# A top-32 threshold from the larger and the smaller of each two scores

## The chip, the cores and the metric

The kernel runs on one core of one Trainium2 chip. The metric is the device time of the whole kernel in microseconds; for the kernel before it is 1531.25 us, the median of 3 runs (1530.28 to 1532.67). A core has five engines that work at the same time, each through its own list of instructions in order: TensorE (PE; the loading of its weights is shown apart as PEld), VectorE (DVE), ScalarE (ACT), GpSimd (POOL), and SyncE (SP), which only starts transfers here. They wait for one another through semaphores. Matrix products land in PSUM; all other tiles lie in SBUF.

## The reference, cut to what matters

```python
def _attn_ref(q, k, v):                      # q, k, v: 8 x 8 x 576 x 64, fp32
    scores = np.matmul(q, k.transpose(0, 1, 3, 2)) / np.sqrt(64)
    kth = np.partition(scores, -32, axis=-1)[..., -32:-31]    # the 32nd largest of each row
    scores = np.where(scores >= kth, scores, -1e9)
    attn = np.exp(scores - np.max(scores, axis=-1, keepdims=True))
    attn = attn / (np.sum(attn, axis=-1, keepdims=True) + 1e-09)
    return np.matmul(attn, v)

def _moe_ref(x, w_in, w_out):                # x: 4608 x 512, w_in: 512 x 2048, w_out: 2048 x 512
    h = x @ w_in
    return (h * np.cos(h)) @ w_out

# reference: attention, heads side by side as 4608 x 512, then _moe_ref
```

For each of 8 x 8 x 576 rows of 576 scores the kernel needs two numbers before it can go on: the largest score and the 32nd largest. Everything below the latter is masked out.

## The kernel before, cut to what matters

A *unit* is 128 rows of tokens for two heads (index `j`), so there are 36 x 4 = 144 units. A unit passes through the engines over several *slots*: in slot `i`, VectorE searches the top 32 of unit `i` (`u`), ScalarE masks and exponentiates unit `i - 1` (`w`), GpSimd normalises unit `i - 2` (`x`), the transfers transpose unit `i - 3` (`y`), and in every second slot TensorE multiplies two older units with the values (`z`). TensorE also makes the scores of unit `i + 1`, and fills its remaining time with the two feed-forward products (`feed`). Each slot gets credit for 4.1 calls of `ff1` or `ff2`. The order of instructions is the program's order. The scores of a unit lie in one PSUM tile of four banks (`sc`, one buffer), and ScalarE copies them to `s` in SBUF.

```python
    def scores(u):
        sc = u["sc"] = ps.tile([P, 2, 2, 512], F32, tag="sc", name="sc", bufs=1)
        for h in range(2):
            for j in range(2):
                d = slice(j * D, (j + 1) * D)
                for b, q0, rows, r0 in u["parts"]:
                    st = pairs[b, u["hp"]]
                    nc.tensor.matmul(
                        sc[r0 : r0 + rows, j, h, 0:HS],
                        st["q"][d, q0 : q0 + rows],
                        st["k"][d, h * HS : (h + 1) * HS],
                        start=True,
                        stop=True,
                    )

    def take_scores(u):
        s = u["s"] = work.tile([P, 2, S], F32, tag="s", name="s", bufs=4)
        nc.scalar.copy(
            out=s.rearrange("p j (h w) -> p (j h) w", h=2),
            in_=u.pop("sc").rearrange("p j h w -> p (j h) w")[:, :, 0:HS],
        )

    def topk_round(u, rnd):
        s = u["s"]
        if rnd == 0:
            u["m8"] = small.tile([P, 2, TOPK], F32, tag="m8", name="m8")
            u["rest"] = work.tile([P, 2, S], F32, tag="rest", name="rest", bufs=1)
        m8, rest = u["m8"], u["rest"]
        src = s if rnd == 0 else rest
        at = slice(8 * rnd, 8 * rnd + 8)
        for j in range(2):
            nc.vector.max(m8[:, j, at], src[:, j])
        if rnd < TOPK // 8 - 1:
            for j in range(2):
                nc.vector.match_replace(rest[:, j], m8[:, j, at], src[:, j], NEG)
        else:
            del u["rest"]

    def bounds(u):

        m8 = u.pop("m8")
        nb = u["nb"] = small.tile([P, 2, 2], F32, tag="nb", name="nb")
        nc.scalar.mul(out=nb, in_=m8[:, :, 0 : TOPK : TOPK - 1], mul=-SCALE)
        nd = u["nd"] = small.tile([P, 2], F32, tag="nd", name="nd")
        for j in range(2):
            nc.scalar.activation(
                out=nd[:, j : j + 1], in_=m8[:, j, TOPK - 1 : TOPK], func=AF.Identity,
                bias=nb[:, j, 0:1], scale=SCALE,
            )
    # ... mask, exponentials, reciprocal, normalise and the rest are cut
```

`nc.vector.max` (MAX8 in the profile) writes the eight largest of a row in descending order. `match_replace` replaces these eight by a very low number; in the profile it is a MATCH_VALUE_LOAD and a MATCH_REPLACE8. Four rounds give the top 32 in order. `bounds` takes the first and the last of the 32.

```python
    def slot(i, u, w, x, y, z):
        if x:
            reciprocal(x)
        if u:
            topk_round(u, 0)
            decode_second(2)
        if w:
            bounds(w)
            mask(w)
            exponentials(w)
        if u:
            topk_round(u, 1)
            topk_round(u, 2)
            topk_round(u, 3)
        take_banks()
        if z:
            values(z)
        if i + 1 < NU:
            scores(units[i + 1])
        if z:
            take_values(z)
        if i + 1 < NU:
            take_scores(units[i + 1])
        for load, b, hp in at_slot.get(i, []):
            load(b, hp)
        load_weights(2)
        if y:
            transposes(y)
        gate(1)
        if x:
            normalise(x)
            split(x)
            write_halves(x)
        feed(2)
        take_banks()
        decode_third()
        decode_first(2)
        reduce_first()
        reduce_second()
        feed(3)
        sines(2)
```

The first 9 slots (`early_slot`) and the last ones (`last_slot`) do the same in another order, without the transfers. `decode_*` are steps on the weights in the first slots. What `feed` calls:

```python
    def ff1(blk, i):
        # ... cut: two blocks of 128 columns, each
            for c in range(NC):
                nc.tensor.matmul(mm[:, at : at + w], w_in[...], blk["xT"][:, c], ...)

    def ff2(blk, i, f0):
        # ... cut
        for f in range(f0, f0 + 2):
            nc.tensor.matmul(o, g[:, at : at + P], w_out[f], start=f == 0, stop=f == NF - 1)
```

Of the kernel before, what the change touches and what calls it, by code (L numbers as in the profile page):

```python
# [10 lines left out]
F32 = mybir.dt.float32  # L11
# [3 lines left out]
AF = mybir.ActivationFunctionType  # L15
ALU = mybir.AluOpType

P = 128
TOPK = 32
NEG = -3.4028234663852886e38  # L20
# [11 lines left out]
def kernel(  # L32
# [9 lines left out]
    nc = tc.nc  # L42
    ctx.enter_context(tc.manual_schedule())
    B, H, D, S = qT.shape
# [6 lines left out]
    HS = S // 2  # L51
    SCALE = 1.0 / math.sqrt(D)
# [3 lines left out]
    consts = ctx.enter_context(tc.tile_pool(name="consts", bufs=1))  # L56
    loads = ctx.enter_context(tc.tile_pool(name="loads", bufs=5))
    work = ctx.enter_context(tc.tile_pool(name="work", bufs=2))
    small = ctx.enter_context(tc.tile_pool(name="small", bufs=4))
# [25 lines left out]
    for i in range(DF // CW):  # L85
        w = consts.tile([P, NC, CW], F32, tag=f"w_in{i}", name=f"w_in{i}")
# [4 lines left out]
    for f in range(NF):  # L91
        w = consts.tile([P, DM], F32, tag=f"w_out{f}", name=f"w_out{f}")
# [62 lines left out]
    units = []  # L155
# [13 lines left out]
    for i in range(2 * NP):  # L169
        t = consts.tile([P, P], F32, tag=f"v_tail{i}", name=f"v_tail{i}")  # L170
# [50 lines left out]
    def take_scores(u):  # L221
        s = u["s"] = work.tile([P, 2, S], F32, tag="s", name="s", bufs=4)
        nc.scalar.copy(  # L223
            out=s.rearrange("p j (h w) -> p (j h) w", h=2),
            in_=u.pop("sc").rearrange("p j h w -> p (j h) w")[:, :, 0:HS],
        )

    def topk_round(u, rnd):
        s = u["s"]
        if rnd == 0:  # L230
            u["m8"] = small.tile([P, 2, TOPK], F32, tag="m8", name="m8")
            u["rest"] = work.tile([P, 2, S], F32, tag="rest", name="rest", bufs=1)
        m8, rest = u["m8"], u["rest"]
        src = s if rnd == 0 else rest
        at = slice(8 * rnd, 8 * rnd + 8)
        for j in range(2):
            nc.vector.max(m8[:, j, at], src[:, j])  # L237
        if rnd < TOPK // 8 - 1:
            for j in range(2):
                nc.vector.match_replace(rest[:, j], m8[:, j, at], src[:, j], NEG)  # L240
        else:
            del u["rest"]

    def bounds(u):

        m8 = u.pop("m8")
        nb = u["nb"] = small.tile([P, 2, 2], F32, tag="nb", name="nb")
        nc.scalar.mul(out=nb, in_=m8[:, :, 0 : TOPK : TOPK - 1], mul=-SCALE)  # L248
        nd = u["nd"] = small.tile([P, 2], F32, tag="nd", name="nd")
        for j in range(2):  # L250
            nc.scalar.activation(
                out=nd[:, j : j + 1], in_=m8[:, j, TOPK - 1 : TOPK], func=AF.Identity,
                bias=nb[:, j, 0:1], scale=SCALE,
            )

    def mask(u):

        s, nb = u["s"], u.pop("nb")
        for j in range(2):
            nc.scalar.activation(  # L260
                out=s[:, j], in_=s[:, j], func=AF.Prelu, bias=nb[:, j, 1:2], scale=SCALE, alpha=FAR
            )
# [63 lines left out]
    def values(us):  # L326


        o = us[0]["o"] = ps.tile([P, 512], F32, tag="mm", name="o", bufs=4)
        for i, u in enumerate(us):  # L330
            pT = u.pop("pT")
            for b, _, rows, r0 in u["parts"]:
                st = pairs[b, u["hp"]]
                r = slice(r0, r0 + rows)
                to = slice(i * P + r0, i * P + r0 + rows)
                for c in range(NT + 1):
                    for j in range(2):
                        d = slice(j * D, (j + 1) * D)
                        if c < NT:
                            lhsT, rhs = st["v"][:, c, d], pT[:, j * (NT + 1) + c, r]  # L340
                        else:
                            lhsT, rhs = st["v_tail"][:, d], pT[:, NT, r]
                        nc.tensor.matmul(o[d, to], lhsT, rhs, start=c == 0, stop=c == NT)  # L343
# [116 lines left out]
    def ff2(blk, i, f0):  # L460
        w = blk["w"]
        if f0 == 0:
            blk["o"] = ps.tile([P, 512], F32, tag="mm", name="o2", bufs=4)
        o = blk["o"]
        per = 1024 // w
        for f in range(f0, f0 + 2):
            g = blk["g"][f // per]
            at = (f % per) * w + i * P
            nc.tensor.matmul(  # L469
                o, g[:, at : at + P], w_out[f], start=f == 0, stop=f == NF - 1  # L470
            )
        if f0 + 2 < NF:
            return
        full.append((take_second, blk, i, o))
# [25 lines left out]
    def feed(n):  # L500

        ff["tick"] += 1
        while n > 0 and ff["credit"] >= 1:
            for kind in (ff["kind"], 1 - ff["kind"]):
                if (can_first, can_second)[kind]():
                    break
            else:
                return
            if kind == 0:
                ff1(*first.popleft())  # L510
            else:
                ff2(*second.popleft())
            ff["kind"] = 1 - kind
            n, ff["credit"] = n - 1, ff["credit"] - 1
# [10 lines left out]
    for n in range(NP, len(order)):  # L525
        i = last[order[n - 5]] - 1 if n >= 5 else 0
        at_slot.setdefault(max(i, NP + 2), []).append((load_qk, *order[n]))
        i = last[order[n - 6]] if n >= 6 else 0
# [8 lines left out]

    EARLY, LAST = 2 * NP, NU - NP

    def early_slot(i, u, w):  # L540
        n = 3 if i < 6 else 2
        topk_round(u, 0)
        decode_second(1 if i == 0 else n)
        scores(units[i + 1])
        for load, b, hp in at_slot.get(i, []):
            load(b, hp)
        load_weights(n)
# [4 lines that stand above are left out]
            reciprocal(w)  # L552
        topk_round(u, 1)
        if i == 0:
# [4 lines that stand above are left out]
            normalise(w)  # L559
# [7 lines that stand above are left out]
        if i != NP:  # L567
            decode_first(n - 1)
        if w:
            transposes_now(w)  # L570
        feed(1)
        decode_first(n - len(wq["second"]))
        if w:
            values([w])
            take_values([w])
# [4 lines that stand above are left out]
        if x:  # L580
            reciprocal(x)
        if u:
            topk_round(u, 0)
            decode_second(2)
        if w:
            bounds(w)
# [6 lines that stand above are left out]
        take_banks()  # L593
        if z:
            values(z)
        if i + 1 < NU:
            scores(units[i + 1])
        if z:
# [22 lines that stand above are left out]
    def last_slot(i, u, w, x, y, z):  # L621
        if x:
            reciprocal(x)
        if u:
            topk_round(u, 0)
            topk_round(u, 1)
        bounds(w)
        mask(w)
        exponentials(w)
        take_banks()  # L630
        sines(1)
# [14 lines that stand above are left out]
        reciprocal(w)  # L646
        normalise(w)
# [3 lines that stand above are left out]
        gate(2)  # L651
        feed(2)
        transposes_now(w)
# [3 lines that stand above are left out]
        feed(1)  # L657
        values([w])
        take_values([w])
        feed(2)  # L660
# [10 lines left out]
    for i in range(NU + 1):  # L671
# [4 lines left out]
        u, w = (units[i - n] if 0 <= i - n < NU else None for n in range(2))  # L676
# [55 lines left out]
```

## Time and profile before

| What | Value |
|---|---|
| median of 3 runs | 1531.25 us |
| span of the profiled execution | 1530.3 us |
| MAX8 over 128 x 576, in all | 1152, mean 752 to 757 ns |
| MATCH_REPLACE8 over 128 x 576, in all | 864, mean 753 ns |
| ScalarE copy of the scores to `s` | 144, mean 1115 ns |
| share of DVE in the chain that ended last | 72% |
| share of PE in that chain | 16% |

How to read it: the page gives busy time by engine, and groups of like instructions with their mean duration. Neighbouring instructions of an engine overlap in the record[...]; what an instruction costs its engine is therefore the distance from its start to the next start. "The chain that ended last" is followed back from the last instruction, at each step to what released it. The timeline lists instructions in order of time, with equal neighbours merged and their number after an x. In a matmul's row the names are output<-inputs, so `mm<-xT,w_in` is `ff1`, `o<-w_out,g` is `ff2`, `sc<-k,q` are the scores and `o<-pT,v` the values. fp32 products show as two matmuls each.

### The profile page before, as it was taken

The numbers are of one execution on the slowest core, as the hardware profiler recorded it, in microseconds if no ns is written. First come the engines' busy times: TensorE is split into PE (matmuls) and PEld (weight loads), VectorE is DVE, ScalarE is ACT, GpSimd is POOL, SyncE is SP. The second block draws the span as 40 slices with busy tenths as digits, with TensorE's granted clock in tenths as the row PEclk, the third lists the DMA queues.
The fourth block names the chain that finished last, engine by engine and source line by source line (L and its number), as shares of the span: only waits on it lengthen the run. The fifth ranks groups of instructions, "written<-read, shape, count | busy, mean of one in ns | idle before, by whom it ended". The sixth has DMA issues, their size and how long they took to land.

```text
span 1530.3 us, 28322 instructions
## 1 busy us (share of the span) xinstructions
PE 1430.3 (93%) x10360; PEld 1022.7 (67%) x10360; DVE 1449.0 (95%) x3102; ACT 1109.6 (73%) x2150; POOL 1105.4 (72%) x838
## 2 busy tenths in 40 slices
PE   4678588999999999999999999999999999999998
PEld 3466266676767676767676767676767676767675
DVE  7999999999999999999999999999999999999911
ACT  7887667777777777777777777777777777777731
POOL 4778957777878787877777777777777778777600
PEclk6588899999999999999999999999999999999999
DMA  8432255645674556655565365645654446444200
GB/s 269 139 96 90 87 152 151 177 116 162 163 178 116 147 133 169 170 132 146 162 170 140 117 162 162 163 131 137 187 148 142 135 131 162 144 136 120 81 8 14
DMA packets 371740, 212.09 MB, mean 139 GB/s; under 512 B 321296, under 2 KB 337937, under 8 KB 371601
## 3 DMA queue, kind: packets, MB, share of 16 engines
q1 hardware_dynamic: 366192, 200.63, 48.4%
q10 hardware_dynamic: 5408, 9.65, 1.7%
q8 instruction: 81, 1.33, 0.4%
q14 instruction: 59, 0.48, 0.1%
HBM read 45.09 MB, written 87.29 MB: 87 GB/s over the span
## 4 chain that ended last, share of the span: by engine, by line
DVE 72%; PE 16%; ACT 5%; issue 5%; DMA 1%; POOL 0%; SPq 0%; ACTq 0%; POOLq 0%; DVEq 0%
DVE m L237 36%; DVE rest L240 33%; PE mm L393 6%; PE o L469 6%; PE o L343 2%; PE sc L213 1%; ACT s L268 1%; ACT s L260 1%; DVE w_out L138 1%; ACT st L127 1%; DVE rden L277 1%; DMA v<-in_v_dram 1%; ACT st L128 0%; PE tp L317 0%; DMA st<-in_moe_w_in_dram 0%
## 5 line engine op out<-in xcount | busy, mean ns | idle before, releaser
L393 PEld LDWEIGHTS mm<-xT,w_in 128*128 128x128 f32 x4608 | 546.6, 193 | 117.0 <-issue 95.2
L237 DVE MAX8 m<-rest 128x8 f32<-128x576 f32 x864 | 613.7, 757 | 0.0
L393 PE MATMUL mm<-xT,w_in 128*128 128x128 f32 x4608 | 567.0, 278 | 19.0 <-ACT xT L349 19.0
L469 PE MATMUL o<-w_out,g 128*128 128x512 f32 x1152 | 539.3, 600 | 11.5 <-POOL g L457 7.5
L240 DVE MATCH_REPLACE8 rest<-m,rest 128x576 f32<-128x576 f32 x576 | 426.4, 753 | 0.0
L469 PEld LDWEIGHTS o<-w_out,g 128*128 128x128 f32 x1152 | 202.7, 191 | 206.2 <-issue 190.7
L294 POOL COPY halves<-s 128x2304 uint16<-128x2304 uint16 x132 | 277.6, 2103 | 85.8 <-DMA rows<-halves 80.1
L282 POOL TENSOR_SCALAR s<-s,rden 128x576 f32<-128x576 f32 x288 | 212.3, 750 | 84.4 <-DVE rden L277 84.4
L268 ACT ACTIVATE s<-s,nd 128x576 f32<-128x576 f32 x288 | 219.5, 763 | 0.6
L240 DVE MATCH_REPLACE8 rest<-m,s 128x576 f32<-128x576 f32 x288 | 213.2, 753 | 0.0
L237 DVE MAX8 m<-s 128x8 f32<-128x576 f32 x288 | 203.1, 752 | 7.0 <-ACT s L223 7.0
L260 ACT ACTIVATE s<-s,nb 128x576 f32<-128x576 f32 x288 | 205.3, 760 | 0.0
L457 POOL TENSOR_TENSOR g<-g,x 128x1024 f32<-128x1024 f32 x68 | 161.4, 2374 | 57.3 <-ACT x L450 57.3
L213 PE MATMUL sc<-k,q 64*128 64x288 f32 (+1 forms) x1280 | 186.9, 439 | 14.5 <-ACT s L223 14.5
L223 ACT COPY s<-sc 128x1152 f32<-128x1152 f32 x144 | 160.6, 1115 | 39.9 <-PE sc L213 39.3
L343 PEld LDWEIGHTS o<-pT,v 128*64 128x64 f32 x2560 | 136.7, 141 | 69.2 <-issue 37.2
L343 PE MATMUL o<-pT,v 128*64 128x128 f32 (+1 forms) x2560 | 165.7, 272 | 14.3 <-ACT pT L321 8.4
L440 POOL TENSOR_TENSOR x<-g,x 128x1024 f32<-128x1024 f32 x68 | 161.3, 2372 | 5.7
L248 ACT ACTIVATE nb<-m 128x4 f32<-128x4 f32 x144 | 29.6, 206 | 185.3 <-DVE m L237 185.3
L405 ACT ACTIVATE g<-mm 128x512 f32<-128x512 f32 x144 | 84.3, 587 | 107.7 <-PE mm L393 107.7
L213 PEld LDWEIGHTS sc<-k,q 64*128 64x128 f32 (+1 forms) x1280 | 101.6, 182 | 66.5 <-ACT s L223 17.6
L431 POOL TENSOR_SCALAR x<-g 128x1024 f32<-128x1024 f32 x68 | 71.1, 1046 | 98.8 <-ACT g L405 94.0
(48 smaller groups left out, 1042.3 us busy)
## 6 DMA issues: line engine op xcount, KB each, us to landing
rows<-halves SPq DMA_DIRECT2D x132, 576.0 KB, 3.2
out_dram<-ob ACTq DMA_DIRECT2D x36, 256.0 KB, 2.1
q<-in_q_dram SPq DMA_DIRECT2D x31, 288.0 KB, 3.1
st<-in_moe_w_in_dram SPq DMA_DIRECT2D x16, 512.0 KB, 5.3
v<-in_v_dram SPq DMA_DIRECT2D x32, 256.0 KB, 3.5
st<-in_moe_w_out_dram SPq DMA_DIRECT2D x16, 512.0 KB, 3.6
k<-in_k_dram SPq DMA_DIRECT2D x31, 144.0 KB, 3.4
k<-in_k_dram SPq DMA_DIRECT2D x32, 128.0 KB, 3.9
```

The source lines that it names most:

```text
L213: nc.tensor.matmul(sc[r0 : r0 + rows, j, h, 0:HS], st["q"][d, q0 : q0 + rows], st["k"][d, h * HS : (h + 1) * HS], start=True, stop=True,)
L237: nc.vector.max(m8[:, j, at], src[:, j])
L240: nc.vector.match_replace(rest[:, j], m8[:, j, at], src[:, j], NEG)
L260: nc.scalar.activation(out=s[:, j], in_=s[:, j], func=AF.Prelu, bias=nb[:, j, 1:2], scale=SCALE, alpha=FAR)
L268: nc.scalar.activation(out=s[:, j], in_=s[:, j], func=AF.Exp, bias=nd[:, j : j + 1], scale=1.0, accum_out=den[:, j : j + 1],)
L282: nc.gpsimd.tensor_scalar(out=s[:, j], in0=s[:, j], scalar1=rden[:, j : j + 1], scalar2=1.0, op0=ALU.mult, op1=ALU.mult,)
L294: nc.gpsimd.tensor_copy(out=halves, in_=s.rearrange("p (k h) -> p h k", h=2))
L343: nc.tensor.matmul(o[d, to], lhsT, rhs, start=c == 0, stop=c == NT)
L393: nc.tensor.matmul(mm[:, at : at + w], w_in[f // FC][:, c, (f % FC) * P : (f % FC + 1) * P], blk["xT"][:, c], start=c == 0, stop=c == NC - 1,)
L440: nc.gpsimd.tensor_tensor(out=x, in0=g, in1=x, op=ALU.subtract)
L457: eng.tensor_tensor(out=g, in0=g, in1=x, op=ALU.mult)
L469: nc.tensor.matmul(o, g[:, at : at + P], w_out[f], start=f == 0, stop=f == NF - 1)
```

## The change

The scores of a row are taken in pairs: score `c` with score `c + 288`. One pass writes the larger of each pair to the first half of `rest`, another the smaller to the second half (`fold`; one operand is read from PSUM, the other from `s`). The top 32 of the larger are searched as before but over 288 elements, in four rounds. A smaller one is in the top 32 only with its larger partner, so at most 16 of the smaller can be: their top 16 are searched in two rounds. Call the lists a1 >= a2 >= ... >= a32 and b1 >= ... >= b16. The 32nd largest of both together is the greatest, over r from 0 to 16, of min(a(32-r), br), where b0 counts as infinite. The list a is therefore written backwards beside b, in `top[..., 0]` and `top[..., 1]`, so that one reduction takes the minima of neighbours (`merge_first`) and another their maximum (`merge_second`). Both merges of a unit run inside the first round of the next unit, between its folds, so that no instruction of the list follows directly on one that it depends on. The largest score is a1.

Units 10 to 141 (132 of 144) fold; the others keep four rounds over 576. The bank of the scores is now released by the second fold instead of by ScalarE's copy. In slots without values, one `feed(1)` is put ahead of the next scores. The purpose is to shorten VectorE's search, whose instructions each scan a whole row.

```diff
--- before.py
+++ after.py
@@ -222,34 +222,95 @@
         s = u["s"] = work.tile([P, 2, S], F32, tag="s", name="s", bufs=4)
         nc.scalar.copy(
             out=s.rearrange("p j (h w) -> p (j h) w", h=2),
-            in_=u.pop("sc").rearrange("p j h w -> p (j h) w")[:, :, 0:HS],
+            in_=u["sc"].rearrange("p j h w -> p (j h) w")[:, :, 0:HS],
         )
+        if not u["folds"]:
+            del u["sc"]
+    def fold(u, op):
+        s, sc = u["s"], u["sc"]
+        if op == ALU.max:
+            u["rest"] = work.tile([P, 2, S], F32, tag="rest", name="rest", bufs=1)
+        else:
+            del u["sc"]
+        i = int(op == ALU.min)
+        nc.vector.tensor_tensor(
+            out=u["rest"][:, :, i * HS : (i + 1) * HS], in0=sc[:, :, 0, 0:HS], in1=s[:, :, HS:S],
+            op=op,
+        )
+    tops = []
+    for i in range(3):
+        t = consts.tile([P, 2, TOPK, 2], F32, tag=f"top{i}", name=f"top{i}")
+        nc.vector.memset(t[:, :, 0, 1], -NEG)
+        tops.append(t)
+    def topk_first(u, w):
+        u["top"] = tops[u["n"] % len(tops)]
+        merges = [merge_first, merge_second] if w and w["folds"] else []
+        if u["folds"]:
+            for op in (ALU.max, ALU.min):
+                fold(u, op)
+                if merges:
+                    merges.pop(0)(w)
+        else:
+            u["rest"] = work.tile([P, 2, S], F32, tag="rest", name="rest", bufs=1)
+        for merge in merges:
+            merge(w)
+        topk_round(u, 0)
 
     def topk_round(u, rnd):
-        s = u["s"]
-        if rnd == 0:
-            u["m8"] = small.tile([P, 2, TOPK], F32, tag="m8", name="m8")
-            u["rest"] = work.tile([P, 2, S], F32, tag="rest", name="rest", bufs=1)
-        m8, rest = u["m8"], u["rest"]
-        src = s if rnd == 0 else rest
-        at = slice(8 * rnd, 8 * rnd + 8)
+        top, rest, lasts = u["top"], u["rest"], TOPK // 8 - 1
+        end = TOPK - 1 - 8 * rnd
+        at = top[:, :, end : end - 8 if rnd < lasts else None : -1, 0]
+        if u["folds"]:
+            search(at, rest[:, :, 0:HS], rest[:, :, 0:HS], rnd < lasts)
+            if rnd < TOPK // 16:
+                low = top[:, :, 1 + 8 * rnd : 9 + 8 * rnd, 1]
+                search(low, rest[:, :, HS:S], rest[:, :, HS:S], rnd < TOPK // 16 - 1)
+        else:
+            search(at, u["s"] if rnd == 0 else rest, rest, rnd < lasts)
+        if rnd == lasts:
+            del u["rest"]
+    def merge_first(u):
+        n = TOPK // 2 + 1
+        u["lesser"] = u["top"].rearrange("p j r i -> p j (r i)")[:, :, 2 * n : 3 * n]
+        nc.vector.tensor_reduce(
+            out=u["lesser"], in_=u["top"][:, :, 0:n], axis=mybir.AxisListType.X, op=ALU.min
+        )
+    def merge_second(u):
+        nc.vector.tensor_reduce(
+            out=u["top"][:, :, TOPK - 1, 1], in_=u.pop("lesser"), axis=mybir.AxisListType.X,
+            op=ALU.max,
+        )
+    def search(to, src, rest, more):
         for j in range(2):
-            nc.vector.max(m8[:, j, at], src[:, j])
-        if rnd < TOPK // 8 - 1:
+            nc.vector.max(to[:, j], src[:, j])
+        if more:
             for j in range(2):
-                nc.vector.match_replace(rest[:, j], m8[:, j, at], src[:, j], NEG)
-        else:
-            del u["rest"]
+                nc.vector.match_replace(rest[:, j], to[:, j], src[:, j], NEG)
 
     def bounds(u):
 
-        m8 = u.pop("m8")
+        ends = u.pop("top").rearrange("p j r i -> p j (r i)")
+        ends = ends[:, :, 2 * TOPK - 2 :] if u["folds"] else ends[:, :, 2 * TOPK - 2 :: 2 - 2 * TOPK]
         nb = u["nb"] = small.tile([P, 2, 2], F32, tag="nb", name="nb")
-        nc.scalar.mul(out=nb, in_=m8[:, :, 0 : TOPK : TOPK - 1], mul=-SCALE)
+        nc.scalar.mul(out=nb, in_=ends, mul=-SCALE)
         nd = u["nd"] = small.tile([P, 2], F32, tag="nd", name="nd")
         for j in range(2):
             nc.scalar.activation(
-                out=nd[:, j : j + 1], in_=m8[:, j, TOPK - 1 : TOPK], func=AF.Identity,
+                out=nd[:, j : j + 1], in_=ends[:, j, 1:2], func=AF.Identity,
                 bias=nb[:, j, 0:1], scale=SCALE,
             )
 
@@ -537,9 +598,13 @@
 
     EARLY, LAST = 2 * NP, NU - NP
 
+    for i, u in enumerate(units):
+        u["n"] = i
+        u["folds"] = EARLY + 2 <= i < LAST + 2
     def early_slot(i, u, w):
         n = 3 if i < 6 else 2
-        topk_round(u, 0)
+        topk_first(u, w)
         decode_second(1 if i == 0 else n)
         scores(units[i + 1])
         for load, b, hp in at_slot.get(i, []):
@@ -580,7 +645,7 @@
         if x:
             reciprocal(x)
         if u:
-            topk_round(u, 0)
+            topk_first(u, w)
             decode_second(2)
         if w:
             bounds(w)
@@ -593,6 +658,8 @@
         take_banks()
         if z:
             values(z)
+        else:
+            feed(1)
         if i + 1 < NU:
             scores(units[i + 1])
         if z:
@@ -622,7 +689,7 @@
         if x:
             reciprocal(x)
         if u:
-            topk_round(u, 0)
+            topk_first(u, w)
             topk_round(u, 1)
         bounds(w)
         mask(w)

```

## The prediction

> **What bounds the kernel now.** I read the shares of busy time first, then the waits of each engine, then the order of instructions inside one slot, then the chain that ended last. The page opens with
>
> ```profile
> PE 1430.3 (93%) x10360; PEld 1022.7 (67%) x10360; DVE 1449.0 (95%) x3102; ACT 1109.6 (73%) x2150; POOL 1105.4 (72%) x838
> ```
>
> Two engines are near the span at once, so a mean share decides nothing. The same busy times cut into stretches of the steady part say more (columns: stretch, its length, then PE, PEld, DVE, ACT and POOL busy, clock, DMA):
>
> ```profile
> 140.00:180.00 40.00, 27.19 (x154) 17.11 (x152) 39.79 (x79) 26.93 (x55) 36.42 (x29) 0.91 0.36 104
> 180.00:240.00 60.00, 44.54 (x332) 30.70 (x332) 60.00 (x132) 40.06 (x84) 36.41 (x29) 0.87 0.57 152
> ...
> 800.00:1000.00 200.00, 197.07 (x1503) 138.26 (x1502) 200.00 (x433) 150.20 (x292) 153.83 (x114) 1.00 0.55 148
> 1000.00:1200.00 200.00, 197.95 (x1423) 143.94 (x1424) 200.00 (x435) 147.26 (x288) 156.33 (x116) 1.00 0.54 144
> ```
>
> VectorE has no idle time at all after 180 us, and the list of its waits holds only the start and the end of the kernel. TensorE is idle for 1 to 1.5%: over 400 to 1400 us its busy time adds up to 987.1 of 1000. Its only wait there is
>
> ```profile
> PE mm L393 <- ACT xT L349: 12.9, 13, 1.3
> ```
>
> 12.9 us, which is just what is missing. So VectorE sets the pace and TensorE follows 1.3% behind the limit. This is the line that decides my number. The timeline of VectorE shows one slot (start, duration, instruction):
>
> ```profile
> 799.87 1.42 DVE L237 MAX8 m<-s 128x8 f32<-128x576 f32 x2
> 801.19 0.09 DVE L240 MATCH_VALUE_LOAD rest<-m,s 128x8 f32 x1
> 801.25 0.76 DVE L240 MATCH_REPLACE8 rest<-m,s 128x576 f32<-128x576 f32 x1
> 801.90 0.10 DVE L240 MATCH_VALUE_LOAD rest<-m,s 128x8 f32 x1
> ...
> 802.63 1.43 DVE L237 MAX8 m<-rest 128x8 f32<-128x576 f32 x2
> ...
> 809.50 0.17 DVE L277 RECIPROCAL rden<-den 128x2 f32<-128x2 f32 x1
> 809.57 1.42 DVE L237 MAX8 m<-s 128x8 f32<-128x576 f32 x2
> ```
>
> The reader should take starts, not durations: the rows overlap. Two MAX8 occupy 801.19 - 799.87 = 1.32, so 0.66 us each (its row says 0.757). A round of two MAX8 and two pairs of value load and replace takes 802.63 - 799.87 = 2.76, so a pair takes (2.76 - 1.32) / 2 = 0.72. Four rounds of which the last has no replaces: 8 x 0.66 + 6 x 0.72 = 9.60; the reciprocal takes 0.07; sum 9.67, and the slot is 809.57 - 799.87 = 9.70. All slots from the 13th to the 141st have this length.
>
> For TensorE's own need I use the end of the chain of waits, where VectorE has nothing left to do (start, us, piece):
>
> ```profile
> 1480.84 1.78 PE mm L393 x16
> 1482.63 1.72 PE o L469 x4
> ...
> 1484.35 1.78 PE mm L393 x16
> ```
>
> One ff1 call is 16 such records (1.78), one ff2 call is 4 (1.72). A slot is credited 4.1 calls, so 4.1 x 1.75 = 7.18. One slot of scores starts at 804.14 and the next matmul at 805.32: 1.18, times 1280 / 1152 for the units that straddle two batches, 1.31. Values start at 801.81 and the scores at 804.14: 2.33 for two units, 1.17 for one. Sum 9.66. The idle share gives 9.70 x 0.987 = 9.58. So TensorE needs 9.58 to 9.66 us of a slot that is 9.70 long.
>
> [...]
>
> **The change part by part.** 132 of 144 units fold (10 to 141).
>
> *Removed* per folded unit: 8 MAX8 and 6 pairs over 576 elements, 9.60 us.
>
> *Added*: the scan of the larger scores, 8 MAX8 and 6 pairs over 288, and of the smaller, 4 MAX8 and 2 pairs over 288. 288 elements cost 0.30 us less than 576[...], so a MAX8 is 0.36 and a pair 0.42: 12 x 0.36 + 8 x 0.42 = 7.68.[...] Merges: 68 elements 0.13 and 34 elements 0.10[...]. Reciprocal 0.07. Sum 9.43 us, against 9.67: **VectorE gains 0.24 to 0.27 us a slot**, 2.6%. Halving the scan saves little, because the number of scans goes from 14 to 20 and two full passes are added.
>
> *Moved*: the 32nd value now appears only after both folds and both merges of the next slot[...]. ScalarE's `bounds` starts then instead of 0.07 us after. From `nb` to the end of `take_scores` its work takes, by the timeline, 5.4 to 6.8 us in even slots and 6.6 to 7.6 us in odd ones, which also copy values. 7.6 + 1.75 = 9.35, still inside 9.43, but with nothing to spare. Before, take_scores was done at least 2.0 us ahead of the slot's end.
>
> *Moved*: the scores bank is held until the second fold, about 1.5 us into the slot, and the next scores need it. They now start 1.4 to 4.9 us into the slot, the earliest ones in even slots. There the change puts one feed-forward call (1.75) ahead of them, so TensorE should not wait for the bank.
>
> *What it is worth.* VectorE could do a slot in 9.43, TensorE not under 9.58 to 9.66. The bound passes to TensorE. Slots 10 to 19 are short of TensorE work (44.5 of 60 us busy), so they get the full gain: 10 x 0.27 = 2.7 us. Slots 20 to 141 fall from 9.70 to about 9.60: 122 x 0.10 = 12 us. The tail after 1450 us is TensorE alone and stays. Sum about 15 us; 1531 - 15 = 1516. I add 1 us for ScalarE's path, now that three engines are within 3% of each other: **1517 us**.
>
> **The rivals.**
> 1. *VectorE stays the bound and the whole 0.27 us comes through*: 132 x 0.27 = 36 us, 1495 us. For it: VectorE is without any gap. Against: TensorE has only 12.9 idle us in 1000, so at most 16 us in the steady part can be had. I give this little.
> 2. *ScalarE's chain becomes the bound.* It begins 1.7 us later, and slots with a table load and two sines have 3.5 us of further work between take_scores and the next `bounds`. If each odd slot were stretched to 9.8, the mean would be 9.7 and the time about 1531. For it: the sum of 9.35 above. Against: ScalarE is idle for a quarter of the time, waiting for `m` about 1.8 us a time (151.8 us in 83 waits between 300 and 1400 us), and most even slots have over 2 us of room.
> 3. *Short instructions cost more than their share.* If each of the 20 scans had 20 ns more of fixed cost (a wait for the result written one instruction earlier is closer now: 0.36 us apart instead of 0.66), VectorE would need 9.43 + 28 x 0.02 = 10.0 with the value loads counted: 132 x 0.3 = 40 us, 1571 at worst. Against: a value load is issued 0.06 us after its predecessor, so issue keeps up, and a value load comes 0.72 us after the MAX8 that it reads, whose row should last 0.757 - 0.30 = 0.46: 0.26 us are left for the result to land.
> 4. *TensorE waits for the fold*, if it gets ahead of VectorE: up to 0.3 us in some slots, some 10 us. The added feed call speaks against it.
>
> **Range and chances.** Were TensorE without any idle time from 180 us on (15.5 us of it before 240 us, 12.9 after 400), the time would be 1531 - 28 = 1503, which is a floor; if rival 2 takes everything, it is 1531. I take 1508 to 1532 as the range for 8 in 10. Faster by 2% means under 1500.6, below that floor, and would need matmuls that take less than I worked out: 0.04. Slower by 2% means over 1561.9, rival 3 at nearly full size: 0.04. Within 2%: 0.92.
>
> **What would show it.** In the profile after: VectorE's first idle time in the steady part, 0.1 to 0.2 us a slot, ended by ScalarE's score copy; TensorE over 99% busy from 400 to 1400 us, and its wait for `xT` nearly gone; MAX8 of 288 elements 0.36 us start to start, the pair 0.42;[...] `nb` starting 1.75 us into a slot; scores later in the slot than before. I am wrong if VectorE still has no gap (then a scan or a fold costs more than worked out, or TensorE needs less), if TensorE shows waits for VectorE's fold, or if the slot is limited by the wait of VectorE for a score copy that itself waited for nothing.

## The result and the profile after

The changed kernel takes 1555.01 us (median of 4 runs, 1554.59 to 1555.13) against 1531.96 us before on the same chip: the ratio is 1.0147, with a 95% interval of 1.0128 to 1.0166. It is 23 us slower; 1517 us was predicted.

The busy times on the page of the changed kernel, and then its chain that ended last by engine:

```profile
PE 1438.8 (93%) x10360; PEld 1026.8 (66%) x10360; DVE 1416.1 (91%) x4689; ACT 1071.0 (69%) x2120; POOL 1105.2 (71%) x838
...
PE 73%; ACT 15%; DVE 7%; DMA 2%; issue 1%; SPq 1%; ACTq 0%; POOL 0%; POOLq 0%; DVEq 0%
```

VectorE's busy time fell by 33 us and it has left the chain (72% before, 7% now). TensorE has taken its place, as predicted. But TensorE is not full. The steady part of the changed kernel, in one stretch (columns as in the prediction):

```profile
400.00:1400.00 1000.00, 975.95 (x7249) 696.58 (x7250) 960.02 (x3352) 706.14 (x1401) 763.73 (x562) 1.00 0.54 147
```

TensorE is now busy for 976 of 1000 us, less than the 987 before, although VectorE no longer holds it back. VectorE is idle for 40 us. The waits of TensorE in the same 1000 us:

```profile
PE mm L454 <- ACT xT L410: 21.9, 13, 1.8
PE o L404 <- DMA pT<-rows: 2.2, 5, 0.6
```

The wait for `xT` comes as often as before (13 times) but is 1.7 us long instead of 1.0. In the timeline VectorE starts a unit every 9.50 us where it does not wait, but slots of 9.9 to 11.0 us lie between. The longest of these, of about 11 us, come back every 8 slots; such a stretch of 8 slots is called a period here. From unit 117 to unit 125 a period takes 1282.42 - 1203.92 = 78.5 us, against 77.6 before.

The chain of waits of the changed kernel, in order of time (start, us, what), shows where a period is decided. `xT` is the transposed result of attention for 128 tokens, which `ff1` reads:

```profile
1210.45 1.17 PE sc L213 x8
1211.62 1.91 PE o L530 x4
1213.54 1.78 PE mm L454 x16
1215.32 5.15 PE o L530 x12
1220.47 1.20 PE sc L213 x8
...
1221.75 1.12 ACT s L223
...
1222.88 1.28 ACT L511
...
1224.18 2.19 ACT x L511 x2
...
1226.98 1.33 ACT s L321 x2
...
1228.33 1.28 ACT L329
...
1229.62 1.64 ACT s L329 x4
...
1231.48 0.59 ACT ob L539
...
1232.47 0.38 ACT xT L410
...
1232.89 1.60 PE mm L454 x12
1234.50 1.72 PE o L530 x4
```

The chain runs along TensorE, piece after piece without a gap, until a unit's scores at 1220.47. There it leaves TensorE for ScalarE: copy of these scores, load of the sine table, two sines, mask, load of the table of exponentials, exponentials, the emptying of a bank of `ff2` (`ob`) and the issue of its transfer, and only then the copy of `xT`. ScalarE does these steps one after the other, in the order shown, and none of them waits for VectorE here. After 1232.89 - 1220.47 = 12.42 us TensorE gets the `xT` for which it has been waiting. Its own timeline shows what it had to do meanwhile:

```profile
1220.40 1.24 PE L213 MATMUL sc<-k,q 64*128 64x288 f32 x8
1221.57 5.42 PE L530 MATMUL o<-w_out,g 128*128 128x512 f32 x12
1226.92 1.09 PE L404 MATMUL o<-pT,v 128*64 128x128 f32 x16
...
1229.26 1.24 PE L213 MATMUL sc<-k,q 64*128 64x288 f32 x8
1230.43 0.71 PE L454 MATMUL mm<-xT,w_in 128*128 128x128 f32 x4
1232.89 1.60 PE L454 MATMUL mm<-xT,w_in 128*128 128x128 f32 x12 [1.76 <-ACT xT L410]
```

That is three feed calls, one pair of values, two sets of scores and the first four records of the next call, 12.42 - 1.76 = 10.66 us of work, and then 1.76 us of nothing. The same place in the kernel before, TensorE and then ScalarE:

```profile
1200.60 1.24 PE L213 MATMUL sc<-k,q 64*128 64x288 f32 x8
1201.77 7.13 PE L469 MATMUL o<-w_out,g 128*128 128x512 f32 x16
...
1214.07 1.60 PE L393 MATMUL mm<-xT,w_in 128*128 128x128 f32 x12 [1.03 <-ACT xT L349]
```

```profile
1204.43 1.15 ACT L450 ACTIVATE x<-x,halfpi 128x1024 f32<-128x1024 f32 x1
1207.43 0.21 ACT L248 ACTIVATE nb<-m 128x4 f32<-128x4 f32 x1 [1.84 <-DVE m L237]
```

There four calls of `ff2` (16 records, 7.1 us) stood behind the scores; one of them now stands ahead. There ScalarE had one sine to do, not two, and waited 1.84 us for VectorE's threshold. By the starts in the two timelines, TensorE's work between these scores and `xT` fell from 1214.07 - 1200.60 - 1.03 = 12.44 us to 1232.89 - 1220.40 - 1.76 = 10.73, and ScalarE's way rose from 1214.07 - 1200.60 - 1.84 = 11.63 (an estimate, as if the threshold had been there) to 12.49. So 0.81 us to spare became a lack of 1.76. The second sine comes with the call too: in the traces of the two kernels without the call (the kernel before, and the first experiment) 17 pairs of sines stand together and 38 sines alone, in the changed kernel and in the kernel before with the call alone 32 pairs and 8.

This closes a loop: TensorE's scores release ScalarE, and ScalarE's `xT` releases TensorE. If TensorE did its 10.66 us faster, it would by this reading only wait longer. A period is TensorE's work, 76.7 us, plus this wait.

So *theory 1* is that the slowdown comes from the added `feed(1)`, through this loop. Its rivals: *theory 2*, that the thresholds come 1.6 us later and hold ScalarE up; *theory 3*, that the scores have to wait for VectorE's folds; and that VectorE's search is simply too dear.

Here is where the 23 us lie, by the starts of units on VectorE in both timelines: the changed kernel is 2.9 us ahead at unit 17, loses 5.1 us up to unit 31, then 16.5 us up to unit 141, and 4.3 us from there to the end.

### The profile page after: what moved, and what is told of

It is laid out like the page before. It is cut to its first block, busy times and chain, and to the rows that moved or that the text cites. A ratio compares the mean times of both kernels' runs of the same rounds, so it can differ in the third digit from the quotient of the medians.

```text
span 1553.3 us, 30144 instructions
## 1 busy us (share of the span) xinstructions
PE 1438.8 (93%) x10360; PEld 1026.8 (66%) x10360; DVE 1416.1 (91%) x4689; ACT 1071.0 (69%) x2120; POOL 1105.2 (71%) x838
## 4 chain that ended last, share of the span: by engine, by line
PE 73%; ACT 15%; DVE 7%; DMA 2%; issue 1%; SPq 1%; ACTq 0%; POOL 0%; POOLq 0%; DVEq 0%
PE mm L454 32%; PE o L530 24%; PE sc L213 8%; PE o L404 8%; DVE top L299 3%; ACT s L329 2%; ACT x L511 2%; DVE rest L302 2%; ACT s L321 2%; ACT L329 1%; ACT s L223 1%; ACT L511 1%; DMA pT<-rows 1%; DVE w_out L138 1%; ACT nd L312 1%
## 5 line engine op out<-in xcount | busy, mean ns | idle before, releaser
L299 DVE MAX8 top<-rest 128x8 f32<-128x288 f32 (+1 forms) x1656 | 681.6, 460 | 0.0
L454 PE MATMUL mm<-xT,w_in 128*128 128x128 f32 x4608 | 569.4, 279 | 29.3 <-ACT xT L410 29.3
L302 DVE MATCH_REPLACE8 rest<-top,rest 128x288 f32<-128x288 f32 (+1 forms) x1104 | 494.9, 456 | 0.0
L239 DVE TENSOR_TENSOR rest<-sc,s 128x576 f32<-128x576 f32 x264 | 198.6, 753 | 52.3 <-ACT s L223 49.1
L309 ACT ACTIVATE nb<-top 128x4 f32<-128x4 f32 x144 | 28.9, 201 | 123.0 <-DVE top L292 122.8
L302 DVE MATCH_VALUE_LOAD rest<-top,rest 128x8 f32 x1104 | 85.6, 77 | 0.0
```

Of the source, the lines that this page charges most:

```text
L239: nc.vector.tensor_tensor(out=u["rest"][:, :, i * HS : (i + 1) * HS], in0=sc[:, :, 0, 0:HS], in1=s[:, :, HS:S], op=op,)
L299: nc.vector.max(to[:, j], src[:, j])
L302: nc.vector.match_replace(rest[:, j], to[:, j], src[:, j], NEG)
L454: nc.tensor.matmul(mm[:, at : at + w], w_in[f // FC][:, c, (f % FC) * P : (f % FC + 1) * P], blk["xT"][:, c], start=c == 0, stop=c == NC - 1,)
```

## The experiments

Each ratio is to the kernel before on the same chip.

### Without the feed call

```diff
         if z:
             values(z)
-        else:
-            feed(1)
```

> The changed kernel without the feed call that it puts ahead of the scores in slots without values. Theory 1: in a stretch of 8 slots TensorE works 76.7 us without a gap and then waits 1.76 us for xT; that wait closes a loop (scores -> ScalarE's score copy, two sines, bounds, mask, exponentials, copy of xT -> TensorE), and the feed call put ahead of the scores takes 1.75 us of work out of it. Without it the wait shrinks to under 0.3 us per 8 slots, 8 slots take 76.7 to 77.0 us and the whole 1520 to 1530 us. Theory 2 (the thresholds come 1.6 us later and hold ScalarE up): little changes, 1548 to 1556 us. Theory 3 (TensorE has to wait for the second fold before it may write scores, and the feed call covers that): slower than the changed kernel, over 1560 us, with waits of the scores for VectorE.

Measured: 1518.94 us, ratio 0.9911 (0.9896 to 0.9926). Without the call the folds are thus a gain of about 13 us; with it the kernel loses 23 us. The waits of TensorE from 400 to 1400 us and the busy times of the same stretch:

```profile
PE mm L454 <- ACT xT L410: 0.2, 1, 0.2
```

```profile
400.00:1400.00 1000.00, 999.51 (x7444) 715.41 (x7444) 987.00 (x3446) 757.18 (x1464) 780.21 (x575) 1.00 0.55 149
```

TensorE is busy 999.5 of 1000 us, so it sets the pace now. Eight slots take 1175.26 - 1098.70 = 76.56 us (units 109 to 117), 9.57 a slot. Theory 3 falls as well: from slot 20 on scores start at the earliest 3.8 us into a slot, while the second fold ends before 1.6 us. Scores wait for VectorE's folds and merges 4 times in either version, all in slots 10 to 15 (14.2 us here, 13.8 in the changed kernel).

Over the whole run the waits for `xT` are 29.3 us in the changed kernel and 3.3 here. That is 26 of the 36 us between the two. Another 6 us are busy time of TensorE (1438.8 against 1432.6), and the rest lies in smaller waits.

### The feed call alone, without folds

```diff
         if z:
             values(z)
+        else:
+            feed(1)
```

in `slot` of the kernel before.

> The kernel before with only the added feed call ahead of the scores in slots without values; no folds. Theory 1: VectorE still paces (9.70 us a slot) and the scores have over 2 us of room before their deadline, so the slot stays 9.70 and the time 1529 to 1536 us, the same as before: the call hurts only where TensorE sets the pace. If the call by itself costs TensorE 1.75 us in every 8 slots whatever VectorE does: 1545 to 1560 us.

Measured: 1555.41 us, ratio 1.0147 (1.0132 to 1.0162): as slow as the whole change. My first expectation missed. I had taken VectorE's 9.70 us for a pace that TensorE would keep to. But the loop has no VectorE in it, and 78.5 us are more than 8 x 9.70 = 77.6, so the loop takes over here too. With the call in place, the folds are worth nothing (1555.41 us without them, 1555.01 with them). Its wait is the same as in the changed kernel:

```profile
PE mm L393 <- ACT xT L349: 21.6, 13, 1.8
PE o L343 <- DMA pT<-rows: 2.7, 5, 0.8
```

### Both merges in the unit's own slot

```diff
-        merges = [merge_first, merge_second] if w and w["folds"] else []
+        merges = []
...
         if rnd == lasts:
             del u["rest"]
+            if u["folds"]:
+                merge_first(u)
+                merge_second(u)
```

> The changed kernel with both merges moved to the end of the unit's own slot, right after its fourth round, so that bounds can start at the slot's start again instead of 1.68 us after it[...]. Theory 2 (late thresholds hold ScalarE up): 8 slots fall to 77 us and the whole to 1522 to 1535 us. Theory 1: in the slot that counts bounds was already 1.7 us later than the merge, held by the sines and they by the scores, so nothing is won: 1549 to 1560 us.

Measured: 1553.64 us, ratio 1.0132 (1.0115 to 1.0149). Within 1.5 us of the changed kernel, with the same wait for `xT` (21.7 us in 1000). `bounds` can now start with the slot, and VectorE's slot is 9.62 us instead of 9.50 where it does not wait. Theory 2 falls.

### The larger half only

```diff
-        nc.vector.memset(t[:, :, 0, 1], -NEG)
+        nc.vector.memset(t, NEG)
+        nc.vector.memset(t[:, :, 0, 1], -NEG)
...
-            if rnd < TOPK // 16:
+            if False:
```

This leaves out the search of the smaller list, so the threshold is that of the larger list alone.

> The changed kernel without the search of the smaller list (4 MAX8 and 2 replaces fewer, some 2.3 us of VectorE's slot); the threshold is then the 32nd of the larger list alone, so this leaves out part of the computation. Folds, merges, the feed call and the order stay. Theory 1: VectorE is not in the loop, so 8 slots still take 78 to 78.6 us and the whole 1545 to 1555 us, with VectorE idle 2 to 2.5 us a slot. If VectorE's work paces the changed kernel: 1555 less up to 132 x 0.3 us, under 1530 us.

Measured: 1553.13 us, ratio 1.0134 (1.0119 to 1.0149). VectorE loses nearly a quarter of its busy time in this stretch (960 us in the changed kernel), and the time stays:

```profile
400.00:1400.00 1000.00, 976.29 (x7234) 696.27 (x7234) 729.76 (x2539) 705.26 (x1403) 765.50 (x563) 1.00 0.53 147
```

VectorE is busy for 730 of 1000 us, TensorE for the same 976. What the search costs does not set the pace of the changed kernel.

### The feed call behind the scores

```diff
         if z:
             values(z)
-        else:
-            feed(1)
         if i + 1 < NU:
             scores(units[i + 1])
         if z:
             take_values(z)
+        else:
+            feed(1)
```

> The changed kernel with the same added feed call, but put right behind the scores instead of ahead of them: the number of feed calls, their groups and the sines stay as in the changed kernel, only TensorE's order of scores and one call differs. Theory 1a (what counts is the TensorE work between the scores and the first matmul that needs the new xT): the loop gets 1.75 us of work back, its wait falls from 1.76 to under 0.4 us per 8 slots, and the whole takes 1517 to 1526 us. Theory 1b (what counts is that the added call lets two sines come together, 1.04 us more of ScalarE's path, in the slot with the wait): 1535 to 1553 us.

Measured: 1522.16 us, ratio 0.9917 (0.9902 to 0.9932). The calls are the same, and ScalarE's list is the same instruction by instruction (2120 in both); only TensorE's order of one call and the scores differs. This is the narrowest test of the cause: the place of 1.75 us of work, not its amount. The wait of TensorE from 400 to 1400 us is nearly gone, with the pairs of sines still there, so theory 1b falls as the whole cause:

```profile
PE mm L454 <- ACT xT L410: 0.8, 4, 0.3
```

### At most one sine in a slot

```diff
-        for _ in range(n):
+        for _ in range(n if ff["end"] else 1):
             blk, g, x, _, scale = waiting.popleft()
```

> The changed kernel, feed call ahead of the scores kept, but at most one sine in a slot: ScalarE's path from the scores to xT is 1.04 us shorter (2.19 us of sines become 1.15), with more table loads in all. Theory 1: the wait per 8 slots falls from 1.76 to 0.6 to 0.9 us and the whole from 1555 to 1535 to 1545 us. If only the place of the feed call counts and ScalarE's path does not: 1550 to 1558 us.

Measured: 1542.13 us, ratio 1.0046 (1.0031 to 1.0061). ScalarE does more in all (it is busy for 1154 instead of 1071 us, and from 400 to 1400 us it has 1470 instructions instead of 1401), and the kernel is 13 us faster than the changed one, because the part of ScalarE's work that lies in the loop is shorter. The wait in its timeline:

```profile
1219.58 0.71 PE L454 MATMUL mm<-xT,w_in 128*128 128x128 f32 x4
1221.19 1.60 PE L454 MATMUL mm<-xT,w_in 128*128 128x128 f32 x12 [0.91 <-ACT xT L410]
```

It is 0.91 us instead of 1.76, just over the expected 0.6 to 0.9. By the chain, ScalarE's `bounds` is here released by VectorE's merge, which ends at 1214.53, and no longer by the end of the sine; so the later threshold takes back a little of the gain. The loop has two sides, and easing either one helps.

### Two calls ahead of the scores

```diff
         else:
-            feed(1)
+            feed(2)
```

> The changed kernel with two feed calls ahead of the scores instead of one (of the same 4.1 a slot). Theory 1: the loop loses another 1.7 us of work, the wait doubles to 3.3 to 3.6 us per 8 slots, and the whole grows by 24 to 28 us to 1577 to 1585 us. If the wait is not set by the work behind the scores: within 8 us of 1555.

Measured: 1729.07 us, ratio 1.1256 (1.1237 to 1.1275). The direction is as expected, the size is far beyond it. The timeline of ScalarE gives one further link, at a place where TensorE then waits for `xT` until 1097.09 (the longest of these waits from 400 to 1400 us is 4.9 us):

```profile
1084.51 1.12 ACT L223 COPY s<-sc 128x1152 f32<-128x1152 f32 x1 [2.22 <-PE sc L213]
1085.53 0.60 ACT L466 ACTIVATE g<-mm 128x512 f32<-128x512 f32 x1
1088.08 0.60 ACT L539 ACTIVATE ob<-o 128x512 f32<-128x512 f32 x1 [1.95 <-PE o L530]
```

ScalarE's order has the emptying of a feed bank between the scores and the sines, and here that bank is filled only by the two calls behind the scores, so ScalarE waits for TensorE inside the loop. From 400 to 1400 us the wait for `xT` is 83.3 us in 19 times, and TensorE waits another 19.0 us for the transposed weights of attention. The mean granted clock of TensorE in this stretch is 0.94, against 1.00 in the changed kernel. ScalarE's list differs too: 64 of the 72 sines stand alone. How much each of these adds is not shown, so this run supports the direction only.

### Without the feed call, merges in the own slot

The edits of the first and the third experiment together.

> The changed kernel without the feed call ahead of the scores and with both merges at the end of the unit's own slot. TensorE is busy 99.95% of the steady part without the feed call alone, so an earlier threshold has nothing left to win there: 1516 to 1522 us, the same as without the feed call alone. If the 1.68 us by which bounds comes later still cost something: under 1514 us.

Measured: 1521.17 us, ratio 0.9908 (0.9894 to 0.9923); the first experiment had 0.9911. So earlier thresholds bring no gain here. But TensorE is not full in this run: VectorE's slot is 9.62 us with the merges at its end, more than the 9.57 that TensorE takes without them, so VectorE sets the pace (busy for 992 of 1000 us) and TensorE waits 3.8 us for `xT`. That an earlier threshold could win next to nothing is shown by the first experiment, where TensorE is idle for only 0.5 of 1000 us.

## Why the prediction was wrong

**What failed** is one step: "There the change puts one feed-forward call (1.75) ahead of them, so TensorE should not wait for the bank", together with the note on the fourth rival, "The added feed call speaks against it." I read the call as free, because the amount of TensorE's work stays the same. I did not ask what was left behind the scores while ScalarE works its way to `xT`, nor what the call does to ScalarE's own list. It takes 1.7 us from TensorE's side of that loop and adds 0.9 us, with a second sine, to ScalarE's; the result is a wait of 1.76 us in each period, which the prediction's sum of 9.58 to 9.66 us a slot doesn't have. Taken out, the time is 1518.94 us, within 2 us of the 1517 predicted; put alone into the kernel before, it makes 1555.41 us. The wait for a fold that it was to prevent does not arise in the steady part without it, and in slots 10 to 15 it arises with the call as well.

**What was right.** *The passing of the bound to TensorE*: 73% of the chain. *TensorE's need of 9.58 to 9.66 us a slot*: 9.57 without the call, and (78.5 - 1.76) / 8 = 9.59 with it. The upper figure takes the scores of units that straddle two batches as longer, which was an estimate; in the kernel before their 16 records take 1.14 us (571.20 to 572.34), the 8 of the others 1.17 (1200.60 to 1201.77). With 1.18 for all the sum is 9.53. *The value of the folds*: about 15 us were worked out, 13 us were measured, but only without the call.

**VectorE's slot** is 9.50 instead of 9.43 us where nothing waits. Its parts in the timeline of the changed kernel:

```profile
808.68 0.76 DVE L239 TENSOR_TENSOR rest<-sc,s 128x576 f32<-128x576 f32 x1 [0.49 <-ACT s L223]
809.35 0.21 DVE L287 TENSOR_REDUCE top<-top 128x34 f32<-128x68 f32 x1
809.48 0.75 DVE L239 TENSOR_TENSOR rest<-sc,s 128x576 f32<-128x576 f32 x1
810.14 0.18 DVE L292 TENSOR_REDUCE top<-top 128x2 f32<-128x34 f32 x1
810.24 0.82 DVE L299 MAX8 top<-rest 128x8 f32<-128x288 f32 x2
810.97 0.08 DVE L302 MATCH_VALUE_LOAD rest<-top,rest 128x8 f32 x1
...
811.81 0.82 DVE L299 MAX8 top<-rest 128x8 f32<-128x288 f32 x2
...
817.98 0.15 DVE L338 RECIPROCAL rden<-den 128x2 f32<-128x2 f32 x1
818.17 0.76 DVE L239 TENSOR_TENSOR rest<-sc,s 128x576 f32<-128x576 f32 x1
```

A fold takes 0.67 from start to start; the merges 0.13 and 0.10, as estimated; a MAX8 over 288 elements (810.97 - 810.24) / 2 = 0.365, against 0.66 over 576; a pair (811.81 - 810.97) / 2 = 0.42, against 0.72. So rival 3, that short instructions cost more than their share, did not come true. (The 0.06 us that it names is the distance from a value load to its replace, 801.19 to 801.25.) From the reciprocal to the first fold there are 818.17 - 817.98 = 0.19 us instead of 0.07. The parts add up to the slot: 2 x 0.67 + 0.23 + 12 x 0.365 + 8 x 0.42 + 0.19 = 9.50. The 9.43 of the prediction, and the 1.75 us after which it has `nb` start, hold the author's estimate for the folds; in the kernel before VectorE reads nothing from PSUM, so no trace of it shows what a fold takes.

**Rival 2**, ScalarE's chain as the bound, came nearest. But I looked for it in a chain that starts at VectorE's thresholds and put its worst at 1531 us. The chain that counts starts at TensorE's scores and ends at TensorE. The prediction said that TensorE's wait for `xT` would be "nearly gone"; that holds without the call (0.2 us) and not with it (21.9 us). The kernel before showed that very line, 12.9 us in 13 waits of 1 us. I took it for mere slack of an engine that is ahead, which it was: ScalarE stood waiting for VectorE's threshold on the way. But it also named the place where a loop would close once its two sides had moved by more than 0.81 us against each other.

## What to carry to other kernels

Moving work within one engine's list is not free merely because its sum stays the same. Before a piece is moved ahead of an instruction that releases another engine, look at what that release leads back to, and add up both sides of that loop (here 12.42 us of ScalarE against 10.66 us left to TensorE). A short wait that recurs at the same place in every period of an engine that is nearly full can mark such a loop, even where it costs nothing yet. When a change has several parts, time each with and without the others, for their effects need not add up: here one line cost 36 us with the folds and 23 us without them, and the folds gained 13 us without that line and nothing with it.

## What the runs showed of the hardware

In the changed kernel the fold, which reads one operand from PSUM and the other from SBUF, takes 0.67 us from start to start for 576 elements (808.68 to 809.35). That is nearly the same as a MAX8 over 576 elements from SBUF in the kernel before (0.66), though that is a different instruction.

A MAX8 over 576 elements took the same time beside an idle and beside a busy GpSimd: in the kernel before, the 132 that ran while GpSimd was idle have rows of 756 ns on average, and so have the 639 during which it was busy for at least 95% of their time.

With two calls ahead of the scores, TensorE was slower after its longest waits. After the wait of 4.85 us that ended at 870.87, twelve records of `ff1` took 2.93 us, and they took the same from 1097.09 on; the mean granted clock was 0.95 from 800 to 1000 us and 0.93 from 1000 to 1200. After the wait of 1.76 us in the changed kernel the granted clock was 1.00 (1232.80 to 1236.00), and twelve such records took 1.60 us.
